# Starting a tile's first matrix product on six of its eight heads: fused top-k attention and two feed-forward networks on one Trainium2 core

## Chip, core and metric

The kernel runs on one core of a Trainium2 chip. The metric is device time in microseconds (us), the median of three runs; less is better. PE is the matrix engine, with PEld its weight loads; DVE, ACT and POOL are the vector, scalar and GpSimd engines, SP the engine that issues most DMAs. PE writes into PSUM banks, which DVE and ACT read; everything else lies in SBUF.

## What is computed

Two batches, 8 heads, 576 rows, head size 64. Each row keeps its 32 largest scores:

```python
scores = scale * np.matmul(q, k.transpose(0, 1, 3, 2))
kth = np.partition(scores, -top_k, axis=-1)[..., -top_k:-top_k + 1]
scores = np.where(scores >= kth, scores, -1000000000.0)
attn = np.exp(scores - np.max(scores, axis=-1, keepdims=True))
attn = attn / (np.sum(attn, axis=-1, keepdims=True) + 1e-09)
x = np.matmul(attn, v)                       # 1152 tokens x 512
h = x @ w1;  x = (np.maximum(h, 0) + np.log1p(np.exp(-np.abs(h)))) @ w2
h = x @ w3;  out = (np.maximum(h, 0) + alpha * np.minimum(h, 0)) @ w4
```

w1 and w3 are 512 x 2048, w2 and w4 2048 x 512. The weights arrive as 64-bit numbers.

## The kernel before

The 1152 tokens are nine tiles of 128 rows, taken in chunks `[[3], [4], [5], [6, 7, 8], [0, 1, 2]]`. The first three chunks are one tile each; their second network is computed together.

**Attention, by tile and head.** `scores` (L455) computes two heads at once on PE into PSUM banks, which ACT copies to SBUF (`s`, L476). `topk` (L485) ranks one head on DVE: four maxima of eight (L480) and three replacements between them (L483). ACT makes the negated, scaled maximum `nb` (L499) and a penalty for all that is under the 32nd value (L508, L509), POOL subtracts it in two halves (L514), and ACT takes the exponential and its sum (L516). `flip` transposes the result in 128x128 blocks on PE (L529, L535), ACT copies them (L532, L536), and `values` multiplies with v (L557). `finish` (L588) runs once all eight heads are there: the inverse sums are spread by POOL and four transposes (L604), and DVE multiplies them into the result (L612).

**Networks.** `Layer` goes through the 2048 hidden columns in 16 blocks of 128. `up` (L640) computes a block `ph` from four slices of x; for the first network ACT computes Abs, Exp and Ln (L663 to L665) and DVE adds (L666). `down` (L683) multiplies the block into `pa`. `up` is two blocks ahead of `down`. Chunks in `NATIVE` use fp32 products (L652, L698); the others split both operands into a high and a low part and use three products (L624 to L626).

**Weights.** `convert` (L341) loads 64-bit weights in two halves into one of `RAWB` raw buffers `cr` (L348), and DVE (L351, L354), ACT (L357, one per half) and POOL (L360, two per half) make 32-bit values `cx` of them. Each is stored to DRAM and loaded again for later chunks. There are 32 units of 1024 columns, sixteen for each network; 15 slots hold weights in SBUF.

**Order.** All operations are recorded with a number, and a table `ORDER` of these numbers, written into the file, is the order in which they are issued; each engine runs its own in that order. `fN` in the table stands for N filler products (L789) on the identity matrix, whose result nobody reads; a `b` behind a number chooses the second of two engines that an operation may run on.

PSUM has few banks: `pacc` 3, `pt` 2 (transposes, spread sums and, after the first tile, scores), `ph` 2, `pav` 1.

Of the kernel before, what the change touches and what calls it, by code (L numbers as in the profile page):

```python
# [18 lines left out]
P = 128  # L19
# [24 lines left out]
XNB = 1  # L44
# [3 lines left out]
RAWB = 2  # L48
RING = 15
NATIVE = {(0, 1), (0, 2), (1, 2), (0, 0)}  # L50
HOLD = {(0, 1): 2, (0, 2): 4}

# [104 lines left out]
109 431 f27 91 124 93 428 92 459 110 94 432 f4 97 125 111 458 118 441 99 112 98 144 100 126 113 135 145 101
127 442 114 146 128 446 158 129 f11 115 147 159 443 447 160 448 148 102 130 444 181 476 116 149 445 f14 131
182 161 133 150 475 460 449 132 151 162 134 f8 136 461 152 157 163 462 203 465 183 463 164 464 137 204 184 138
466 494 153 f10 139 477 467 174 185 141 140 478 468 f4 154 495 165 479 186 155 226 480 166 205 481 227 187 482  # L160
167 511 206 168 188 483 169 207 484 189 242 f26 170 172 485 228 171 190 512 173 208 243 f4 175 191 229 196 177
197 496 192 198 497 176 199 f2 178 209 498 230 219 501 499 210 231 500 179 180 244 502 f11 193 211 530 200 513
503 194 265 201 514 212 266 504 531 245 515 232 213 518 202 516 246 f18 380 517 214 381 233 519 374 547 382
# [136 lines left out]
def topk_attention_moe_kernel(ctx: ExitStack, tc: tile.TileContext, q, k, v, w1, w2, w3, w4, alpha, out):  # L300
# [541 lines left out]
```

## Time and profile before

| | us |
|---|---|
| median of three runs | 664.43 (663.53 to 664.88) |
| profiled execution, its own time | 661.64 |
| its span, first to last instruction | 659.8 |
| PE busy, of it fillers | 643.9, 59.5 |
| DVE busy | 542.9 |
| ACT busy | 496.9 |
| POOL busy | 377.0 |

The time of an execution is 1.8 us more than its span. Busy time of PE is modelled: a product's end overlaps the next one's start, so the distance between starts is the price of a product. The idle time given in front of an instruction names what ended it. The granted clock of the profile is a share of 2.4 GHz.

### The profile page before, as it was taken

The page shows a single profiled execution, that of the slowest core. Times are in us where ns is not written, and L with a number is a line of the kernel's source. Part 1 is how long each engine was busy: PE and PEld are TensorE (multiplying, and loading weights), DVE is VectorE, ACT ScalarE, POOL GpSimd, SP SyncE. Part 2 cuts the span into 40 slices and gives each one's busy share as a digit, 9 for nine tenths or more (in the row PEclk, how much of TensorE's full clock was granted, in tenths as well). Part 3 has the DMA queues.
Part 4 walks back from the last instruction along what each step waited for, and adds up shares of the span by engine and source line. Part 5 has one row for each costly group of instructions (what it writes and reads, how often), then busy time and mean ns, then how long its engine had stood idle before and what let it go on. Part 6 is the DMA issues. An engine that isn't in the chain of part 4 may idle for free.

```text
span 659.8 us, 12350 instructions
## 1 busy us (share of the span) xinstructions
PE 643.9 (98%) x4330; PEld 500.2 (76%) x4330; DVE 542.9 (82%) x1046; ACT 496.9 (75%) x1118; POOL 377.0 (57%) x402
## 2 busy tenths in 40 slices
PE   9999997999999899999999999999999999999997
PEld 7899765667677555555567788779898999999886
DVE  5999999999999999999998889999734654664632
ACT  4878898998799988788788889888545667673432
POOL 2566765642343677887585769886644343742520
PEclk9999999999999999999999999999999999999999
DMA  8765777740044379858424222221243433432501
GB/s 298 257 212 210 242 253 241 241 164 1 1 136 137 112 217 311 290 167 266 155 80 147 94 97 96 65 97 58 79 133 125 146 118 129 160 128 96 160 1 48
DMA packets 30159, 98.46 MB, mean 149 GB/s; under 512 B 3473, under 2 KB 4241, under 8 KB 30097
## 3 DMA queue, kind: packets, MB, share of 16 engines
q1 hardware_dynamic: 29952, 97.54, 45.2%
q8 instruction: 34, 0.56, 0.4%
q14 instruction: 29, 0.23, 0.1%
q10 hardware_dynamic: 144, 0.13, 0.1%
HBM read 78.52 MB, written 19.14 MB: 148 GB/s over the span
## 4 chain that ended last, share of the span: by engine, by line
PE 87%; issue 4%; POOL 3%; ACT 2%; DMA 2%; DVE 1%; SPq 0%; POOLq 0%; DVEq 0%
PE ph L652 11%; PE pa L698 10%; PE scrap L789 9%; PE ph L624 7%; PE pa L624 7%; PE ph L626 7%; PE ph L625 7%; PE pa L625 7%; PE pa L626 7%; PE pss L471 6%; PE pp L529 4%; POOL cx L360 2%; DMA cr<-in_w_dram 2%; POOL e L514 1%; PE pav__3750 L557 1%
## 5 line engine op out<-in xcount | busy, mean ns | idle before, releaser
L370 POOL TENSOR_TENSOR w<-w,wh 128x512 fp32r<-128x512 f32 x82 | 126.3, 1550 | 101.4 <-ACT wh L393 93.8
L514 POOL TENSOR_TENSOR e<-s,e 128x288 f32<-128x288 f32 x144 | 121.0, 860 | 64.4 <-ACT e L509 58.6
L480 DVE MAX8 m<-r 128x8 f32<-128x576 f32 x216 | 155.7, 747 | 0.1
L360 POOL TENSOR_TENSOR cx<-cx,cr 128x256 int32<-128x256 int32 x128 | 94.1, 762 | 62.2 <-ACT cr L357 60.5
L483 DVE MATCH_REPLACE8 r<-m,r 128x576 f32<-128x576 f32 x144 | 106.4, 742 | 0.0
L698 PE MATMUL pa<-cx,g 128*128 128x512 f32 x188 | 92.9, 604 | 2.3 <-DVE g L666 2.3
L357 ACT ACTIVATE cr<-cr 128x512 int16<-128x512 uint32 x64 | 82.5, 1378 | 4.4 <-DVE cr L354 4.0
L393 ACT CAST wh<-w 128x1024 fp32r<-128x1024 f32 x64 | 66.8, 1045 | 6.3 <-PE pa L624 2.0
L476 ACT COPY s<-pss 128x288 f32<-128x288 f32 x144 | 53.3, 407 | 21.7 <-PE pss L471 21.2
L480 DVE MAX8 m<-s 128x8 f32<-128x576 f32 x72 | 52.8, 749 | 10.6 <-ACT s L476 10.5
L789 PEld LDWEIGHTS scrap<-ident 128*128 128x128 f32 x474 | 55.9, 195 | 6.7 <-issue 5.3
L789 PE MATMUL scrap<-ident 128*128 128x128 f32 x474 | 59.5, 282 | 1.4 <-POOL ident masks.py:199 1.4
L516 ACT ACTIVATE e<-e,nb 128x576 f32<-128x576 f32 x72 | 55.8, 776 | 5.7 <-POOL e L514 5.5
L624 PE MATMUL pa<-w,gh 128*128 128x512 f32 x144 | 59.0, 409 | 0.0
L371 DVE TENSOR_TENSOR w<-w,wh 128x512 fp32r<-128x512 f32 x46 | 37.2, 811 | 26.4 <-ACT wh L393 24.8
L625 PE MATMUL pa<-wh,gl 128*128 128x512 f32 x144 | 56.8, 395 | 0.0
L626 PE MATMUL pa<-wh,gh 128*128 128x512 f32 x144 | 56.8, 395 | 0.0
L670 ACT ACTIVATE g<-ph 128x384 f32<-128x384 f32 x48 | 23.4, 490 | 43.7 <-PE ph L626 37.7
L471 PE MATMUL pss<-ks,q 64*64 64x288 f32 x576 | 53.1, 432 | 2.5 <-ACT pt L532 2.2
L672 DVE SCALAR_TENSOR_TENSOR g<-g,rest,ph 128x384 f32<-128x384 f32 x48 | 29.2, 608 | 31.8 <-ACT g L670 31.7
L371 DVE TENSOR_TENSOR gl<-g,gh 128x384 fp32r<-128x384 f32 x41 | 42.2, 1029 | 15.2 <-ACT gh L679 14.8
L652 PEld LDWEIGHTS ph<-xh,cx 128*128 128x128 f32 x336 | 42.0, 191 | 15.8 <-issue 8.2
(131 smaller groups left out, 1461.6 us busy)
## 6 DMA issues: line engine op xcount, KB each, us to landing
w<-ws SPq DMA_DIRECT2D x67, 512.0 KB, 3.3
cr<-in_w_dram SPq DMA_DIRECT2D x64, 512.0 KB, 5.5
ws<-cx SPq DMA_DIRECT2D x32, 512.0 KB, 6.6
v<-in_v_dram SPq DMA_DIRECT2D x12, 320.0 KB, 6.3
ks<-in_k_dram SPq DMA_DIRECT2D x11, 288.0 KB, 5.1
q<-in_q_dram SPq DMA_DIRECT2D x8, 256.0 KB, 5.3
out_dram<-o SPq DMA_DIRECT2D x8, 256.0 KB, 2.5
ks<-in_k_dram SPq DMA_DIRECT2D x2, 144.0 KB, 2.4
```

Source lines behind the costliest of these rows:

```text
L360: op("POOL", lambda part=part, r=r, cs=cs: nc.gpsimd.tensor_add(part().bitcast(I32)[:, cs], part().bitcast(I32)[:, cs], r().bitcast(I32)[: ...
L370: lambda: nc.gpsimd.tensor_sub(lo(), x(), hi().bitcast(F32)),
L471: nc.tensor.matmul(pss[n]()[part], qr()[head, pair, part], ks()[head, cs], start=True, stop=True)
L480: op("DVE", lambda: nc.vector.max(out=out(), in_=x()), reads=reads, writes=writes)
L483: op("DVE", lambda: nc.vector.match_replace(out=out(), in_to_replace=found(), in_values=x(), imm_value=LOWEST), reads=reads, writes=writes)
L514: op("POOL", lambda cs=cs: nc.gpsimd.tensor_sub(e()[:, cs], s()[:, cs], e()[:, cs]), reads=[s], writes=[e])
L624: nc.tensor.matmul(acc, ah, b_l, start=first, stop=False)
L625: nc.tensor.matmul(acc, a_l, bh, start=False, stop=False)
L626: nc.tensor.matmul(acc, ah, bh, start=False, stop=last)
L652: nc.tensor.matmul(hp(), w[0]().bitcast(F32)[:, cs], self.x[c][0]()[:, c, :], start=c == 0, stop=c == KT - 1)
L698: nc.tensor.matmul(acc(), gh()[:, cs], w[0]().bitcast(F32), start=first, stop=last)
L789: plan.emit(ORDER, lambda: nc.tensor.matmul(scrap()[:, :P], ident, ident, start=True, stop=True))
```

## The change

It begins the first network of tile 3 when six of its eight heads are ranked. `finish_part` takes over from `finish` for this tile, once after head 5 and once after head 7, each with its own sums, and writes three and then one of the four slices of x. `Layer.ahead` multiplies the first three slices with all 16 blocks of the first matrix, four blocks to a PSUM bank, and ACT copies the half sums to SBUF (`h`). Later `up_block` adds the half sum by a product with the identity, and the fourth slice.

For single tiles in fp32 (`wide`, two), two blocks of the first network share a PSUM bank and one set of activations of 256 columns. A third raw weight buffer is there. `nb` may be computed on POOL. Attention of the last chunk is recorded after the first network of the chunk before, and the last tile's results are copied in another split. The table is new: 239 fillers instead of 237, and 37 of the 72 `nb` on POOL; six of the low parts of `g` moved from DVE to POOL, four penalties from DVE to ACT.

```diff
-RAWB = 2
+RAWB = 3
+STREAM = 6
...
 ORDER = """
-4 2 5 3 12 364 363 386 387 240 f5 6 7 8 f1 9 11 10 19 96 56 f3 195 95 156 40 77 f4 13 26 41 117 14 0 42 27 15 f3
...
@@ topk
-        if h == 0:
+        if h == 0 or streamed(ci) and h == STREAM:
...
-        op("ACT", lambda: nc.scalar.mul(nb(), m()[:, 0:1], -SCALE), reads=[m], writes=[nb])
+        op(("ACT", "POOL"), (lambda: nc.scalar.mul(nb(), m()[:, 0:1], -SCALE), lambda: nc.gpsimd.tensor_scalar(
+            nb(), m()[:, 0:1], -SCALE, None, op0=ALU.mult)), reads=[m], writes=[nb])
@@ values
+        if streamed(ci):
+            if h in (STREAM - 1, H - 1):
+                finish_part(ci, t, h)
+        elif h == H - 1:
             finish(ci, ti, t)
+    def finish_part(ci, t, h):
+        lo = STREAM if h == H - 1 else 0
+        n = h + 1 - lo
+        ks = slice(lo // 2, (h + 1) // 2)
...
+        op("POOL", lambda: nc.gpsimd.tensor_copy(
+            rx()[:, lo:h + 1], rs()[:, lo:h + 1].unsqueeze(2).broadcast_to([P, n, D])), reads=[rs], writes=[rx])
+        op("PE", spread, reads=[rx], writes=[pr])
+        op("ACT", lambda: nc.scalar.copy(xn()[:, cols], pr()[:, cols]), reads=[pr], writes=[xn])
+        op("DVE", lambda: nc.vector.tensor_tensor(
+            x()[:, ks].rearrange("p k n -> p (k n)"), av()[:, cols], xn()[:, cols], op=ALU.mult),
...
@@ Layer.__init__
+            self.wide = GROUP if self.native and layer == 0 and self.n == P else 1
+            self.early = streamed(ci) and layer == 0
+            if self.early:
+                self.sums = [buf("row", OB, [P, DM], F32, f"h{i}") for i in range(FJ // 4)]
+                for j in range(FJ):
+                    if j % GROUP == 0:
+                        fetch((layer, j // GROUP, 0), j, ci, True)
+                    if j % 4 == 0:
+                        z = bank("pacc", 3, 4 * P, f"pe{j // 4}")
+                    self.ahead(j, z)
+        def ahead(self, j, z):
+            lo = j % 4 * P
+            self.products(j, j, z, slice(lo, lo + P), 0, STREAM // 2, [z], True)
+            if j % 4 == 3:
+                o = self.sums[j // 4]
+                op("ACT", lambda: nc.scalar.copy(o(), z()),
+                   reads=[z], writes=[Half(o, i * P, i * P + P) for i in range(4)])
+        def up_block(self, j, at):
+            n, nm, ci = self.n * self.wide, f"{self.layer}{self.ci}_{j}", self.ci
+            if self.early:
+                hp, o = bank("ph", 2, n, f"ph{nm}"), self.sums[j // 4]
+                for i in range(self.wide):
+                    k, cols = (j + i) % 4 * P, slice(i * P, (i + 1) * P)
+                    self.products(j + i, at + i, hp, cols, STREAM // 2, KT, [hp], False, Half(o, k, k + P))
+                self.activate(j, at, n, nm, ci, hp, [hp])
+                return
...
@@ products, called by ahead and up_block
+                    if base is not None:
+                        nc.tensor.matmul(hp()[:, cols], ident, base(), start=True, stop=False)
...
@@ the loop over chunks
-        if ci + 1 < len(CHUNKS):
+        follows = ci + 1 < len(CHUNKS) and min(len(CHUNKS[ci]), len(CHUNKS[ci + 1])) > 1
+        if ci + 1 < len(CHUNKS) and not follows:
             attend(first_row[ci + 2] - 1)
         for layer in (0, 1) if among[ci][-1] == ci else (0,):
+            if layer and follows:
+                attend(first_row[ci + 2] - 1)
```

Three places of the issue order, as the built programs have it. Names carry numbers of buffers: `pp`, `pq` are transposes of ranked heads, `pss` scores, `pr` spread sums, `pav` values, `ph`, `pa` blocks and sums of a network, `pe` half sums, `py` the transposed output of the first network, `cr` raw and `cx` converted weights.

**PE, the end of tile 3's attention**, around the spread of its sums (`pr`). Before:

```order
L789 MATMUL scrap<-ident 128x128 x11
L529 MATMUL pp_883<-ident,e_71 128x128 x4
L604 MATMUL pr__893<-ident,rx_847 128x128 x4
L789 MATMUL scrap<-ident 128x128 x18
L652 MATMUL ph_1_939<-xh_917,cx_208 128x128 x4
L652 MATMUL ph_0_948<-xh_917,cx_208 128x128 x4
L535 MATMUL pq_962<-ident,e_71 128x128
L529 MATMUL pp_966<-ident,e_71 128x128 x4
```

and in the change, from just ahead of the transposes of tile 3's last two heads on:

```order
L875 MATMUL scrap<-ident 128x128 x6
L527 MATMUL pp_763<-ident,e_72 128x128 x4
L613 MATMUL pr__772<-ident,rx_696 128x128 x3
L875 MATMUL scrap<-ident 128x128 x7
L727 MATMUL pe_797<-xh_785,cx_343 128x128 x3
L527 MATMUL pp_804<-ident,e_72 128x128 x4
L533 MATMUL pq_810<-ident,e_72 128x128
L727 MATMUL pe_797<-xh_785,cx_343 128x128 x3
L727 MATMUL pe_797<-xh_785,cx_472 128x128 x6
L727 MATMUL pe_830<-xh_785,cx_220 128x128 x6
L727 MATMUL pe_830<-xh_785,cx_249 128x128 x6
L727 MATMUL pe_858<-xh_785,cx_519 128x128 x6
```

Fillers before the first products went from 18 to 7, and the products of the first three slices stand there, ahead of tile 3's last values; other fillers stand later.

**ACT, the same stretch**, from the last transposes of tile 3 on. Before:

```order
L532 COPY pt_74<-pp_796 128x512
L536 COPY pt_74<-pq_801 128x128
L499 ACTIVATE nb_811<-m_768 128x1
L476 COPY s_835<-pss_820 128x288
L516 ACTIVATE e_71,sum_841<-e_71,nb_639 128x576
L476 COPY s_845<-pss_817 128x288
L357 ACTIVATE cr_699<-cr_699 128x512 x2
L476 COPY s_845<-pss_851 128x288
L476 COPY s_835<-pss_854 128x288
L508 ACTIVATE kb_888<-m_683 128x1
L509 ACTIVATE e_71<-s_555,kb_888 128x576
L532 COPY pt_73<-pp_883 128x512
```

and in the change:

```order
L354 ACTIVATE cr_590<-cr_590 128x512 x2
L694 COPY h_836<-pe_797 128x512
L534 COPY pt_74<-pq_810 128x128
L354 ACTIVATE cr_670<-cr_670 128x512 x2
L694 COPY h_864<-pe_830 128x512
L506 ACTIVATE kb_871<-m_707 128x1
L507 ACTIVATE e_71<-s_564,kb_871 128x576
L530 COPY pt_74<-pp_804 128x512
L694 COPY h_896<-pe_858 128x512
L473 COPY s_911<-pss_890 128x288
L473 COPY s_914<-pss_893 128x288
```

Two conversions (four halves) and the half sums stand close together, and by the end of the piece ACT has done eighteen halves, where it had done sixteen.

**PE and ACT, the start of the second network for tiles 3 to 5.** PE before:

```order
L578 MATMUL py_2722<-ident,o_2690 128x128 x4
L529 MATMUL pp_2738<-ident,e_72 128x128 x4
L652 MATMUL ph_1_2749<-yh_1704,cx_2692 128x384 x4
L652 MATMUL ph_0_2780<-yh_1704,cx_2692 128x384 x4
L529 MATMUL pp_2803<-ident,e_72 128x128 x4
L535 MATMUL pq_2811<-ident,e_72 128x128
L652 MATMUL ph_3_2813<-yh_1704,cx_2247 128x384 x4
```

PE in the change:

```order
L580 MATMUL py_2526<-ident,o_2518 128x128 x4
L556 MATMUL pav__2112<-pt_74,v_1434 64x128 x10
L468 MATMUL pss_2552<-ks_747,q_1692 64x288 x2
L468 MATMUL pss_2555<-ks_747,q_1692 64x288 x2
L727 MATMUL ph_0_2561<-yh_1621,cx_2160 128x384 x2
L727 MATMUL ph_1_2568<-yh_1621,cx_2160 128x384 x4
L468 MATMUL pss_2587<-ks_747,q_1692 64x288 x2
L468 MATMUL pss_2590<-ks_747,q_1692 64x288 x2
L727 MATMUL ph_0_2561<-yh_1621,cx_2160 128x384 x2
L641 MATMUL pr__2607<-ident,rx_2488 128x128 x4
L527 MATMUL pp_2616<-ident,e_71 128x128 x4
L727 MATMUL ph_3_2623<-yh_1621,cx_2213 128x384 x4
L527 MATMUL pp_2648<-ident,e_71 128x128 x4
```

ACT in the change, from the copy of `py` on:

```order
L585 COPY yh_1621<-py_2526 128x4x128
L354 ACTIVATE cr_2327<-cr_2327 128x512 x2
L514 ACTIVATE e_71,sum_2490<-e_71,nb_2393 128x576
L473 COPY s_2571<-pss_2555 128x288
L473 COPY s_2575<-pss_2552 128x288
L354 ACTIVATE cr_2418<-cr_2418 128x512 x2
L748 ACTIVATE g_1_2597<-ph_1_2568 128x384
L473 COPY s_2571<-pss_2590 128x288
L473 COPY s_2575<-pss_2587 128x288
L354 ACTIVATE cr_2467<-cr_2467 128x512 x2
L748 ACTIVATE g_0_2632<-ph_0_2561 128x384
L496 ACTIVATE nb_2638<-m_2627 128x1
L530 COPY pt_73<-pp_2616 128x512
```

The transposes `pp` no longer follow `py` directly: values, scores and two of the second network's blocks come between, and ACT does six conversion halves there.

## Rows read from the trace of the kernel before

**Rows 1.** The page's head and its busy time, share and instructions by engine.

```profile
span 659.8 us, 12350 instructions
...
PE 643.9 (98%) x4330; PEld 500.2 (76%) x4330; DVE 542.9 (82%) x1046; ACT 496.9 (75%) x1118; POOL 377.0 (57%) x402
```

**Rows 2.** The page's costliest groups: busy us, mean ns, then idle before.

```profile
L789 PE MATMUL scrap<-ident 128*128 128x128 f32 x474 | 59.5, 282 | 1.4 <-POOL ident masks.py:199 1.4
```

**Rows 3.** Windows by stage, three answers; columns as in the first line.

```profile
core 0: us, PE busy (x) PEld busy (x) DVE busy (x) ACT busy (x) POOL busy (x), PEclk, DMA share, GB/s
...
78.00:125.00 47.00, 39.22 (x383) 26.73 (x384) 45.88 (x100) 43.51 (x111) 31.34 (x42) 1.00 0.78 253
...
235.00:505.00 270.00, 269.68 (x1615) 192.11 (x1614) 237.95 (x462) 215.39 (x462) 194.25 (x201) 1.00 0.45 146
...
53.00:80.00 27.00, 26.94 (x261) 24.17 (x260) 26.64 (x55) 21.49 (x42) 19.10 (x24) 1.00 0.72 240
80.00:140.00 60.00, 52.26 (x481) 35.41 (x480) 58.88 (x129) 57.23 (x152) 37.49 (x49) 1.00 0.76 243
...
80.00:114.10 34.10, 27.98 (x284) 18.97 (x283) 32.98 (x71) 32.37 (x86) 21.53 (x28) 1.00 0.77 251
```

**Rows 4.** The chain that ended last: start us, us, what, with its count of records.

```profile
150.77 0.86 PE pa L698 x2
...
154.39 1.24 PE pav__1588 L557 x20
...
158.67 0.65 PE pss L471 x8
...
160.82 0.87 PE pp L529 x8
...
181.67 1.78 PE ph L652 x16
...
253.24 2.58 PE ph L652 x8
```

**Rows 5.** Timeline of PE, two waits: start us, us, instruction, [idle before <-releaser].

```profile
113.14 1.05 PE L652 MATMUL ph<-xh,cx 128*128 128x128 f32 x7 [2.19 <-DVE g L666]
...
229.72 0.63 PE L529 MATMUL pp<-ident,e 128*128 128x128 f32 x4 [2.04 <-ACT s L476]
```

**Rows 6.** Windows of 1 us around the clock's fall, columns as in rows 3.

```profile
230.00:231.00 1.00, 1.00 (x6) 0.59 (x4) 1.00 (x2) 1.00 (x2) 1.00 (x2) 0.91 0.00 0
231.00:232.00 1.00, 1.00 (x3) 0.67 (x2) 1.00 (x5) 0.97 (x4) 0.86 (x2) 0.50 0.00 0
```

**Rows 7.** Timeline: PE's last transpose of three pairs of heads, and DVE's last maximum.

```profile
114.14 0.27 PE L535 MATMUL pq<-ident,e 128*128 128x128 f32 x1
...
132.07 1.40 DVE L480 MAX8 m<-r 128x8 f32<-128x576 f32 x2
...
140.14 0.27 PE L535 MATMUL pq<-ident,e 128*128 128x128 f32 x1
...
221.86 0.27 PE L535 MATMUL pq<-ident,e 128*128 128x128 f32 x1
```

**Rows 8.** Groups of ACT from 78 to 145 us by shape, then three of the whole run.

```profile
L357 ACT ACTIVATE cr<-cr 128x512 int16<-128x512 uint32 x14 | 18.0, 1381 | 1.5 <-DVE cr L354 1.3
L532 ACT COPY pt<-pp 128x512 f32<-128x512 f32 x11 | 6.6, 603 | 0.2
...
L663 ACT ACTIVATE g<-ph 128x128 f32<-128x128 f32 x19 | 5.0, 282 | 1.3 <-PE ph L652 1.3
...
L499 ACT ACTIVATE nb<-m 128x1 f32<-128x1 f32 x11 | 2.3, 209 | 0.0
...
L670 ACT ACTIVATE g<-ph 128x384 f32<-128x384 f32 x48 | 23.4, 490 | 43.7 <-PE ph L626 37.7
...
L514 POOL TENSOR_TENSOR e<-s,e 128x288 f32<-128x288 f32 x144 | 121.0, 860 | 64.4 <-ACT e L509 58.6
...
L829 POOL MEMSET const-float32-1.0<- 128x1 f32 x1 | 0.1, 98 | 0.0
```

More of the change, by code (lines that the diff above doesn't have):

```diff
@@ L157 @@
[L157 to L161, printed above, removed]
@@ L487, in topk @@
         ci, ti, t, h = rows[i]
-        if h == 0:
-            tiles[t]["sum"] = buf("sum", 2, [P, H], F32, f"sum{t}")
-        total = tiles[t]["sum"]
+        if h == 0 or streamed(ci) and h == STREAM:
+            tiles[t]["sum"] = buf("sum", 2, [P, H], F32, f"sum{t}{h}")
+        total = work[i]["sum"] = tiles[t]["sum"]
         s = work[i].pop("s")
@@ L547, in values @@
         av, pts = tiles[t]["av"], pt_tiles[i // 2 % PB]
+        o0 = h // 2 * P
         pt = pts[0].tile
@@ L558, in products @@
                                          start=c == 0, stop=c == 4)
-        op("PE", products, reads=[*pts] + [vt for vt, _, _ in parts], writes=[av])
-        if h == H - 1:
+        op("PE", products, reads=[*pts] + [vt for vt, _, _ in parts], writes=[Half(av, o0, o0 + P)])
+        if streamed(ci):
+            if h in (STREAM - 1, H - 1):
+                finish_part(ci, t, h)
+        elif h == H - 1:
             finish(ci, ti, t)
     def features(name, ci, layer):
-        tag = name + str(ci % 2) * (not layer)
         n = sum(len(CHUNKS[c]) for c in (among[ci] if layer else [ci])) * P
+        tag = name + (f"s{ci % 2}" if n == P else "") * (not layer)
         if (layer, ci) in NATIVE:
@@ L586, in to_features, with streamed, spread @@
                reads=[pp, hi], writes=[lo])
+    def streamed(ci):
+        return ci == 0 and STREAM
+    def finish_part(ci, t, h):
+        lo = STREAM if h == H - 1 else 0
+        n = h + 1 - lo
+        ks = slice(lo // 2, (h + 1) // 2)
+        if not lo:
+            x = features("x", ci, 0)[0]
+            xs[ci] = [(x, f"x{c}") for c in range(KT)]
+        x = xs[ci][0][0]
+        av, total = tiles[t]["av"], work[rows.index((ci, 0, t, h))]["sum"]
+        rs = buf("rs", 2, [P, H], F32, f"rs{t}{h}")
+        op("DVE", lambda: nc.vector.tensor_scalar(rs()[:, lo:h + 1], total()[:, lo:h + 1], 1e-9, None, op0=ALU.add),
+           reads=[total], writes=[rs])
+        op("DVE", lambda: nc.vector.reciprocal(rs()[:, lo:h + 1], rs()[:, lo:h + 1]), writes=[rs])
+        xn = buf("xn", XNB, [P, DM], F32, f"xn{t}{h}")
+        rx = buf("rx", 1, [P, H, D], F32, f"rx{t}{h}")
+        pr = bank("pt", 2, KT * P, f"pr{t}{h}_")
+        cols = slice(ks.start * P, ks.stop * P)
+        def spread():
+            for c in range(ks.start, ks.stop):
+                nc.tensor.transpose(pr()[:, c * P:(c + 1) * P], rx()[:, 2 * c:2 * c + 2, :].rearrange("p a b -> p (a b)"), ident)
+        op("POOL", lambda: nc.gpsimd.tensor_copy(
[4 more added lines that the diff above has]
+            x()[:, ks].rearrange("p k n -> p (k n)"), av()[:, cols], xn()[:, cols], op=ALU.mult),
+           reads=[Half(av, c * P, c * P + P) for c in range(ks.start, ks.stop)] + [xn] + [x] * (lo > 0),
+           writes=[f"x{c}" for c in range(ks.start, ks.stop)] + [x] * (lo == 0))
     def finish(ci, ti, t):
@@ L591, in finish @@
         av, total = tiles[t]["av"], tiles[t]["sum"]
+        avs = [Half(av, o, o + P) for o in range(0, KT * P, P)]
         parts, cs = xs[ci], slice(ti * P, (ti + 1) * P)
@@ new lines, in ahead @@
+        def ahead(self, j, z):
[5 more added lines that the diff above has]
+                   reads=[z], writes=[Half(o, i * P, i * P + P) for i in range(4)])
+        def up(self, j, at):
+            if at % self.wide:
+                return
+            self.up_block(j, at)
+        def up_block(self, j, at):
[6 more added lines that the diff above has]
+                self.activate(j, at, n, nm, ci, hp, [hp])
+                return
+            hp = bank("ph", 2, n, f"ph{nm}")
+            for i in range(self.wide):
+                self.products(j + i, at + i, hp, slice(i * self.n, (i + 1) * self.n), 0, KT, [hp])
+            self.activate(j, at, n, nm, ci, hp, [hp])
@@ L644, in up, with products @@
+        def products(self, j, at, hp, cols, c_lo, c_hi, writes, ahead=False, base=None):
+            n, ci = self.n, self.ci
             w = [x.parts[j % GROUP] for x in ready[self.layer, j // GROUP, 0]]
-            hp = bank("ph", 2, n, f"ph{nm}")
-            step = 1 if at == 0 and self.x[0] is not self.x[-1] else 2
-            for c0 in range(0, KT, step):
+            step = c_hi - c_lo if ahead else 1 if at == 0 and self.x[0] is not self.x[-1] or (c_hi - c_lo) % 2 else 2
+            for c0 in range(c_lo, c_hi, step):
@@ L651, in products, with activate @@
                         if self.native:
-                            nc.tensor.matmul(hp(), w[0]().bitcast(F32)[:, cs], self.x[c][0]()[:, c, :],
-                                             start=c == 0, stop=c == KT - 1)
+                            nc.tensor.matmul(hp()[:, cols], w[0]().bitcast(F32)[:, cs], self.x[c][0]()[:, c, :],
+                                             start=base is None and c == 0, stop=c == c_hi - 1)
                         else:
                             xh, xl, *_ = self.x[c]
-                            three(hp(), w[0]()[:, cs], w[1]()[:, cs], xh()[:, c, :], xl()[:, c, :],
+                            three(hp()[:, cols], w[0]()[:, cs], w[1]()[:, cs], xh()[:, c, :], xl()[:, c, :],
                                   c == 0, c == KT - 1)
-                op("PE", products,
-                   reads=w + [x for c in range(c0, c0 + step) for x in self.x[c][-2:]], writes=[hp])
+                op("PE", products if not ahead else lambda f=products: f(),
+                   reads=w + [x for c in range(c0, c0 + step) for x in self.x[c][-2:]] + [base] * (base is not None),
+                   writes=writes)
+        def activate(self, j, at, n, nm, ci, hp, made):
             g = buf("g", GB, [P, n], F32, f"g{nm}")
             if self.layer == 0:
-                op("ACT", lambda: nc.scalar.activation(g(), hp(), AF.Abs), reads=[hp], writes=[g])
+                op("ACT", lambda: nc.scalar.activation(g(), hp(), AF.Abs), reads=made, writes=[g])
                 op("ACT", lambda: nc.scalar.activation(g(), g(), AF.Exp, scale=-1.0), writes=[g])
@@ L724, in down @@
             half = DM // 2
-            for o, acc in zip(os, self.acc):
-                if self.layer == 1 and ci == len(CHUNKS) - 1:
-                    op("ACT", lambda o=o, acc=acc: nc.scalar.copy(o()[:, :half], acc()[:, :half]),
-                       reads=[acc], writes=[Half(o, 0, half)])
-                    z = o if o is not os[-1] else buf("row", OB, [P, DM], F32, f"oz{nm}")
-                    op("DVE", lambda z=z, acc=acc: nc.vector.tensor_copy(
-                        z()[:, half:], acc()[:, half:]), reads=[acc], writes=[Half(z, half, DM)])
-                else:
-                    op("ACT", lambda o=o, acc=acc: nc.scalar.copy(o(), acc()), reads=[acc],
-                       writes=[Half(o, 0, half), Half(o, half, DM)])
+            final = self.layer == 1 and ci == len(CHUNKS) - 1
+            for i, (o, acc) in enumerate(zip(os, self.acc)):
+                whole = [Half(o, 0, half), Half(o, half, DM)]
+                if not final or i == 0:
+                    op("ACT", lambda o=o, acc=acc: nc.scalar.copy(o(), acc()), reads=[acc], writes=whole)
+                elif i < len(os) - 1:
+                    op("DVE", lambda o=o, acc=acc: nc.vector.tensor_copy(o(), acc()), reads=[acc], writes=whole)
+                else:
+                    t, z = self.tiles[i], buf("row", OB, [P, DM], F32, f"oz{nm}")
+                    op("ACT", lambda o=o, acc=acc: nc.scalar.copy(o()[:, :half], acc()[:, :half]),
+                       reads=[acc], writes=whole)
+                    op("ACT", lambda t=t, o=o: nc.scalar.dma_start(out[t * P:(t + 1) * P, :half], o()[:, :half]),
+                       reads=whole)
+                    op("DVE", lambda z=z, acc=acc: nc.vector.tensor_copy(z()[:, half:], acc()[:, half:]),
+                       reads=[acc], writes=[Half(z, 0, half), Half(z, half, DM)])
+                    op("SP", lambda t=t, z=z: nc.sync.dma_start(out[t * P:(t + 1) * P, half:], z()[:, half:]),
+                       reads=[Half(z, 0, half), Half(z, half, DM)])
             for ti, (t, o) in enumerate(zip(self.tiles, os)):
@@ L737, in down @@
                     to_features(o, bank("pacc", 3, 512, f"py{nm}{ti}"), ys[group[-1]][0], before + ti)
-                elif ci < len(CHUNKS) - 1 or o is not os[-1]:
+                elif not final or ti < len(os) - 1:
                     op("SP", lambda t=t, o=o: nc.sync.dma_start(out[t * P:(t + 1) * P, :], o()),
                        reads=[Half(o, 0, half), Half(o, half, DM)])
-                else:
-                    op("ACT", lambda t=t, o=o: nc.scalar.dma_start(out[t * P:(t + 1) * P, :half], o()[:, :half]), reads=[Half(o, 0, half)])
-                    op("SP", lambda t=t, z=z: nc.sync.dma_start(out[t * P:(t + 1) * P, half:], z()[:, half:]), reads=[Half(z, half, DM)])
     steps = []
```

183 lines of the change are left out of this document (112 added, 71 removed), and 103 rows, old and new, of the table ORDER.

## The prediction

> **What bounds the kernel now.** I read the page's busy table first. PE is busy 98% of the span [rows 1], but 59.5 us of that is work that computes nothing: 237 filler products, two records each [rows 2]. The windows by stage [rows 3] show the rest. The fillers stand before 78 us, where DVE still ranks the scores. From 78 to 125 us PE is idle 47.00 - 39.22 = 7.8 us, in waits like the 2.19 us one in [rows 5]. From 235 to 505 us it is idle 0.3 us in 270 [rows 3], so every microsecond won or lost before that arrives at the end whole. There is one more loss: at 229.72 PE has waited 2.04 us for ACT's copy of scores [rows 5], and the granted clock, 1.00 until 230, is then 0.50 (1.2 instead of 2.4 GHz) until past 234. One window at 0.91, three at 0.50 and one at 0.88 (the first two are in [rows 6]) cost 0.09 + 1.50 + 0.12 = 1.7 us. That place loses 2.04 + 1.7 = 3.75 us. So the bound is PE's order of work, held up by ACT and DVE between 78 and 235 us.
>
> **The change, part by part.** PE prices are starts, not the modelled ends: a 128-column fp32 product costs 2 x 0.111 = 0.222 us, a 512-column one 0.86, a 384-column one 2 x 0.3225 = 0.645, ten value products 1.24, four score products 0.65, a transpose 0.109 [rows 4].
>
> *Added PE work.* Sixteen products add the saved half sums back into PSUM: 16 x 0.222 = 3.6 us. Two fillers more: 0.4 us. All other products are the same in number. Together +4.0 us, and since PE has no idle time after 235 us nothing covers them there.
>
> *Where PE stands.* I compare at one point, the transposes of heads 2 and 3 of tile 5, at 140.14 before [rows 7]. Up to it the order of the change has 88 products of the first matrix instead of 74 (+3.1 us), one 512-column product more (+0.86), the sixteen additions and the two fillers: +8.0 us of PE work. So behind it stands 4.0 us less than before. When is the point reached? Three bounds:
> - PE alone: 140.1 - 7.8 of waits + 8.0 = 140.3.
> - DVE: its last maximum for this pair ends at 133.5 [rows 7]. Its order now holds one more replacement before that and wider additions, about 1 us more; subtracting on POOL and two ACT steps take another 4 us: not before 138.5.
> - ACT: by the transposes of heads 6 and 7 of tile 4 (114.14 before, [rows 7]) it has five more halves of weight conversions, 5 x 18.0/14 = 6.4 us, four copies of half sums at 0.60, one more copy of transposes 0.60 and one more ranked head 1.0, less seven small scalings at 0.21 that moved to POOL [rows 8]. Its activations come out even: 30 of 128 columns before, 22 of 256 now, which I put half way from 0.28 for 128 to 0.49 for 384 columns [rows 8]. That is +9.0 us. ACT worked 32.4 us between 80 and 114.1 [rows 3]; 32.4 + 9.0 at its share of 57.2/60 between 80 and 140 takes 43.4 us, so 123.4. PE's products from there to the point come to 18.4 us in the new order; from 140.14 to 221.86 before [rows 7] products of 77.5 us took 81.7, of which 0.6 was idle, so 4.5% more: 19.2 and 142.6.
>
> I take 141.9, near ACT's bound, because ACT has the least room there. That is 1.8 later than before, with 4.0 less to do.
>
> *The loss at 229.* Before, these transposes (heads 2 and 3 of tile 7) stand right behind the last ones of the first network's output. In the new order 5.2 us of the second network's 384-column products and 3 us of other work come between, and the pair of heads ahead of them already stands behind 19.5 us more of PE work, so what DVE ranks for them is done in time. But ACT now has six conversion halves (7.7 us) in the stretch that follows, and about 5.8 us of smaller work: 13.5 us, against 11.2 us of PE work up to the second set of transposes there, which needs a PSUM buffer that ACT empties. The new wait lies between 0 and 2.3 us; I take 1.4, since ACT starts this stretch with some lead.
>
> *At nothing.* The third raw buffer lets weight loads start earlier; but DVE, which takes them up, is busy 58.9 of the 60 us from 80 to 140 [rows 3], so at most 1.1 us of waiting for them can go there, and PE gains it only where DVE is its bound, which it isn't above. The 37 scalings moved to POOL: the nearest rows are a 128x1 memset of 0.098 us and the subtraction of 288 columns, 0.86 [rows 8], so 3.6 to 32 us of POOL, which is idle 43% of the span [rows 1]; I take the low end, by size. They stand in front of subtractions of older heads, and wait for DVE instructions one or two ahead: cover is DVE's backlog. Six low parts moved from DVE to POOL, in a stretch in which neither holds PE. The last copies are split anew over ACT and DVE; within 0.3 us either way.
>
> **Sum.** +1.8 - 4.0 - (3.75 - 1.4) = -4.55 us on the profiled execution (span 659.8, time 661.64). That one lies 2.8 us under the median of 664.43; the difference carries over: **659.9 us**. A measurement can tell 0.2%, 1.3 us, from no change.
>
> **Rivals.**
> 1. *No new wait.* The point at 140.3 and no loss in the second network: +0.2 - 4.0 - 3.75 = -7.55, 656.9 us. For it: in the old order PE waits 0.3 us in the 270 after 235 [rows 3], so waits are no rule there. Against: ACT's queue, as above. Chance 0.14.
> 2. *PE has room.* If added products slip into time in which PE only seems busy, the 4.0 us cost nothing: -8.55, 655.9 us. For it: weight loads fill 192 of 270 us between 235 and 505 [rows 3]. Against: a pair of 512-column records takes its 0.86 us from start to start [rows 4], with nothing left between. The Trainium skill (Perfetto Trace Analysis, Identifying the Most-Contended Engine) calls matmul busy time a poor measure of room on TensorE and wants the busy share of weight loads instead. By that rule 29% of this stretch would be free, and this rival would hold. Chance 0.08.
> 3. *The loss in the second network returns whole*: a wait of 2.3 us and the clock at half again, 1.7, with the point at ACT's 142.6: +2.5 - 4.0 - 3.75 + 4.0 = -1.25, 663.2 us, no change that can be told. For it: the conversions are packed there, and a wait of 2.04 us was enough before. Chance 0.15.
> 4. *ACT falls behind between 80 and 125 us*, slower than before. The scores, transposes and spread sums rotate through two PSUM buffers that ACT empties, so PE waits for ACT, and ACT for PE. If ACT reaches only its share of 53 to 80 us, 21.5/27 = 0.80 [rows 3], its 41.4 us take 51.8: 131.8, the point at 151.0, and +10.9 - 4.0 - 2.35 = +4.55, 669.0 us. It decides at a share of 0.88, where the sum is nought. For it: nine more microseconds in the same queue. Against: the share was low at 53 to 80 because ACT had nothing to do. Chance 0.18.
>
> **Numbers.** The forecast has 0.45; with rivals 1 and 2 faster has 0.67, rival 3 is no change 0.15, slower 0.18. The range starts under rival 2, at 655.5, and ends at 667, an ACT share of 0.83; it leaves out the end of rival 4 and little below.
>
> **What would show it.** Right: the transposes of heads 2 and 3 of tile 5 at 140 to 143 us; idle of PE between 78 and 142 under 5 us; the granted clock at 1.00 past 220, or a dip that follows a wait near the second network's start; products after that point without gaps; 16 more products of 0.222 us. The forecast fails if that point comes after 146 us with ACT under 0.88 busy from 80 us on (rival 4), if a wait of over 4 us stands behind 235 us, or if the added products don't lengthen PE's work (rival 2).

## The result and the profile after

The changed kernel takes 672.40 us (median of 4 runs, 671.23 to 673.55), the kernel before on the same chip 664.65 (4 runs, 663.53 to 665.37): ratio 1.0131, interval 1.0107 to 1.0155. It is slower; the forecast was 659.9 us and its range ended at 667.0. The profiled execution took 673.37 us, span 671.6: 11.7 us more than the one of before, where the medians differ by 7.75.

These lines of the page of the changed kernel (its head, the busy time, and the fillers' group) are to be set beside [rows 1, 2].

```profile
span 671.6 us, 12322 instructions
...
PE 646.3 (96%) x4366; PEld 505.3 (75%) x4366; DVE 537.9 (80%) x1014; ACT 488.7 (73%) x1021; POOL 396.3 (59%) x446
...
L875 PE MATMUL scrap<-ident 128*128 128x128 f32 x478 | 61.2, 284 | 1.3 <-POOL ident masks.py:199 1.3
```

Work did not grow on DVE or ACT; PE lost time. Windows of the changed kernel, columns as in [rows 3]:

```profile
78.00:125.00 47.00, 34.42 (x302) 27.16 (x301) 33.85 (x70) 31.86 (x69) 23.86 (x35) 0.85 0.65 211
80.00:100.00 20.00, 8.50 (x85) 7.64 (x85) 13.64 (x28) 6.96 (x14) 5.90 (x7) 0.66 0.53 171
...
235.00:505.00 270.00, 264.91 (x1649) 185.53 (x1648) 247.25 (x475) 215.75 (x464) 193.92 (x221) 1.00 0.40 130
```

From 78 to 125 us PE is idle 12.6 us instead of 7.8, and in 80 to 100 every engine stands: DVE, full before [rows 3], has 13.64 of 20. PE's three largest waits in the whole run (waited for: us in total, times, longest):

```profile
PE pav__1010 L556 <- DVE xh L619: 11.5, 1, 11.5
PE ph L727 <- DVE g L750: 1.8, 1, 1.8
PE pp L527 <- ACT s L473: 1.5, 3, 0.6
```

One wait of 11.5 us stands out. The timeline around it, in the order PE, DVE, ACT (start us, us, instruction, [idle before <-releaser]):

```profile
92.97 2.40 PE L556 MATMUL pav__1010<-pt,v 128*64 128x64 f32 x40 [11.50 <-DVE xh L619]
95.30 3.18 PE L875 MATMUL scrap<-ident 128*128 128x128 f32 x16
98.41 0.71 PE L468 MATMUL pss<-ks,q 64*64 64x288 f32 x8
...
91.98 0.75 DVE L477 MAX8 m<-r 128x8 f32<-128x576 f32 x1
92.65 0.27 DVE L619 TENSOR_TENSOR xh<-pav__442,xn 128x128 f32<-128x128 f32 x1
92.84 0.07 DVE L480 MATCH_VALUE_LOAD r<-m,r 128x8 f32 x1
92.91 0.73 DVE L480 MATCH_REPLACE8 r<-m,r 128x576 f32<-128x576 f32 x1
102.80 1.42 DVE L477 MAX8 m<-s 128x8 f32<-128x576 f32 x2 [9.16 <-ACT s L473]
...
78.62 0.27 ACT L618 COPY xn<-pr__975 128x128 f32<-128x128 f32 x1 [0.19 <-PE pr__975 L613]
99.24 0.70 ACT L473 COPY s<-pss 128x288 f32<-128x288 f32 x2 [12.26 <-PE pss L468]
```

The rows read like this. Tile 4's first value products (pav__1010) want the one PSUM bank for value sums, in which tile 3's still stand (pav__442). The last reader is the DVE multiplication for tile 3's heads 6 and 7, a step the change split off. Its other operand xn was copied by 78.89 us, but on DVE fourteen ranking steps of tile 4's heads and six conversion instructions still stand ahead of it, and it runs at 92.65. PE stands from 81.47 on. The scores of the next heads are behind the value products on PE, so ACT gets none to copy (12.26 us) and DVE, once through its queue, none to rank (9.16 us). When PE goes on it has half its clock (granted 0.50, 1.2 GHz): 40 value products take 2.40 us, where experiment 1 below shows the same 40 in 1.39 at 1.00.

In the kernel before, one multiplication ended the whole tile, well ahead of the next tile's value products:

```profile
76.11 0.69 DVE L612 TENSOR_TENSOR xh<-pav__419,xn 128x512 f32<-128x512 f32 x1
...
83.15 1.03 PE L557 MATMUL pav__1001<-pt,v 128*64 128x64 f32 x28
```

The next rows are the transposes of three pairs of heads in the changed kernel: heads 2 and 3 of tile 4, heads 6 and 7 of it, and heads 2 and 3 of tile 5. Before, the last two were at 114.14 and 140.14 [rows 7].

```profile
106.90 0.27 PE L533 MATMUL pq<-ident,e 128*128 128x128 f32 x1
...
133.76 0.27 PE L533 MATMUL pq<-ident,e 128*128 128x128 f32 x1
...
154.82 0.27 PE L533 MATMUL pq<-ident,e 128*128 128x128 f32 x1
```

So the point of comparison comes at 154.82 instead of the predicted 141.9.

### The profile page after: what moved, and what is told of

The parts are those of the page before. It is cut to its first block, busy times and chain, and to the rows that moved or that the text cites. A ratio compares the mean times of both kernels' runs of the same rounds, so it can differ in the third digit from the quotient of the medians.

```text
span 671.6 us, 12322 instructions
## 1 busy us (share of the span) xinstructions
PE 646.3 (96%) x4366; PEld 505.3 (75%) x4366; DVE 537.9 (80%) x1014; ACT 488.7 (73%) x1021; POOL 396.3 (59%) x446
## 4 chain that ended last, share of the span: by engine, by line
PE 76%; ACT 11%; DVE 6%; issue 4%; POOL 2%; DMA 1%; SPq 0%; POOLq 0%; DVEq 0%; ACTq 0%
PE pa L777 9%; PE ph L727 8%; PE ph L661 7%; PE scrap L875 7%; PE ph L662 7%; PE ph L663 7%; PE pa L661 6%; PE pa L663 6%; PE pa L662 6%; PE pss L468 5%; ACT cr L354 3%; PE pp L527 3%; DVE m L477 2%; DVE r L480 2%; ACT e L507 1%
## 5 line engine op out<-in xcount | busy, mean ns | idle before, releaser
L367 POOL TENSOR_TENSOR w<-w,wh 128x512 fp32r<-128x512 f32 x82 | 124.0, 1520 | 95.1 <-ACT wh L390 87.1
L512 POOL TENSOR_TENSOR e<-s,e 128x288 f32<-128x288 f32 x144 | 119.1, 844 | 64.3 <-ACT e L507 42.0
L357 POOL TENSOR_TENSOR cx<-cx,cr 128x256 int32<-128x256 int32 x128 | 104.0, 834 | 42.3 <-ACT cr L354 35.4
L354 ACT ACTIVATE cr<-cr 128x512 int16<-128x512 uint32 x64 | 84.5, 1379 | 8.0 <-DVE cr L351 7.8
L875 PE MATMUL scrap<-ident 128*128 128x128 f32 x478 | 61.2, 284 | 1.3 <-POOL ident masks.py:199 1.3
L875 PEld LDWEIGHTS scrap<-ident 128*128 128x128 f32 x478 | 57.6, 198 | 6.5 <-issue 5.0
L507 ACT ACTIVATE e<-s,kb 128x576 f32<-128x576 f32 x68 | 52.8, 777 | 2.3
L777 PEld LDWEIGHTS pa<-cx,g 128*128 128x128 f32 x192 | 32.5, 190 | 28.6 <-issue 23.2
```

The costliest lines, as they stand in the source:

```text
L354: op("ACT", lambda r=r: nc.scalar.activation(r().bitcast(I16)[:, :, 2], r()[:, :, 0], AF.Copy, scale=2.0 ** -29), reads=[part], writes=[r])
L357: op("POOL", lambda part=part, r=r, cs=cs: nc.gpsimd.tensor_add(part().bitcast(I32)[:, cs], part().bitcast(I32)[:, cs], r().bitcast(I32)[: ...
L367: lambda: nc.gpsimd.tensor_sub(lo(), x(), hi().bitcast(F32)),
L512: op("POOL", lambda cs=cs: nc.gpsimd.tensor_sub(e()[:, cs], s()[:, cs], e()[:, cs]), reads=[s], writes=[e])
L777: nc.tensor.matmul(acc(), gh()[:, cs], w[0]().bitcast(F32), start=first, stop=last)
L875: plan.emit(ORDER, lambda: nc.tensor.matmul(scrap()[:, :P], ident, ident, start=True, stop=True))
```

## The experiments

In the expectations theory A is the explanation just given, or the one that the prediction stands on; rivals B and C are others.

**1. The multiplication early.** One number of the table, the late multiplication's 208, moves:

```diff
-238 476 f3 223 200 565 254 224 518 f3 221 529 222 271 f4 247 530 ...
+238 476 f3 223 200 565 254 224 518 f3 221 529 222 208 271 f4 247 530 ...
-... 278 572 f10 260 208 555 603 293 262 483 569 604
+... 278 572 f10 260 555 603 293 262 483 569 604
```

> The changed kernel with one table entry moved: the DVE multiplication that ends tile 3's heads 6 and 7 (xh<-pav,xn 128x128) stands 19 DVE instructions earlier, right behind the conversion that began at 79.45 us, instead of at 92.65 us; xn was there at 78.89. Theory A, the single pav bank is freed late by DVE's own order: PE's wait of 11.5 us before tile 4's first value products shrinks to under 1 us, DVE's idle time of 9.2 us behind it goes too, the transposes of heads 2 and 3 of tile 4 (106.9 before this edit) come at 94 to 98, and 671.6 us becomes 659 to 662. Rival B, DVE or ACT is simply late by that much and the wait only shows it: the same time is waited for at the next transposes, which stay at 103 or later, and the whole at 669 or more. Rival C, PE is let through and then waits for first layer weights whose raw loads are late: a wait on cx or cr of several us at 95 to 110, and 664 to 667.

659.77 us (6 runs, 658.09 to 660.46), ratio to before 0.9933 (0.9906 to 0.9961). Windows and rows of PE in this kernel (the last three are again the transposes of the three pairs):

```profile
80.00:100.00 20.00, 18.71 (x224) 16.37 (x226) 20.00 (x40) 18.20 (x39) 14.87 (x20) 1.00 0.88 308
...
80.00:123.40 43.40, 41.36 (x383) 30.05 (x382) 42.97 (x88) 41.50 (x91) 31.82 (x44) 1.00 0.83 290
...
82.26 1.39 PE L556 MATMUL pav__1011<-pt,v 128*64 128x64 f32 x40
83.58 2.05 PE L875 MATMUL scrap<-ident 128*128 128x128 f32 x16
85.56 0.72 PE L468 MATMUL pss<-ks,q 64*64 64x288 f32 x8
...
94.44 0.27 PE L533 MATMUL pq<-ident,e 128*128 128x128 f32 x1
...
121.33 0.27 PE L533 MATMUL pq<-ident,e 128*128 128x128 f32 x1
...
142.38 0.27 PE L533 MATMUL pq<-ident,e 128*128 128x128 f32 x1
```

This is theory A, number for number: the wait is gone, DVE is full, the transposes of heads 2 and 3 of tile 4 come at 94.44, and the kernel becomes 0.7% faster than the one before. One instruction's place on DVE was worth 12.6 us. The wait is 11.5 of it, and the clock adds 2.1: from the value products to the scores PE needs 98.41 - 92.97 = 5.44 us in the changed kernel and 85.56 - 82.26 = 3.30 here, for the same work. The point of comparison differs by 154.82 - 142.38 = 12.4, about 1 us less than these two together. Most of that is no gain: this profile came to the value products 0.8 us later, at 82.26 where PE began to wait at 81.47 in the other.

**2. Half as far.** The same number leaves its old place as in experiment 1, but goes here:

```diff
-532 289 288 240 f8 226 257 273 550 533 290 274 241 228 ...
+532 289 288 240 f8 226 257 273 550 533 290 274 208 241 228 ...
```

> The same DVE multiplication moved only half as far: it stands behind the second maximum of head 4 of tile 4, where DVE was at 86.6 us in the changed kernel. Theory A: PE's wait before tile 4's first value products is 5 to 6 us instead of 11.5, and the time lies 5 to 6 us under the changed kernel's, 665 to 667 us. Rival B (the wait only shows a lateness of DVE or ACT): within 1 us of the changed kernel, 671 to 673.

665.99 us (10 runs, 665.04 to 668.35). PE's longest wait is:

```profile
PE pav__1010 L556 <- DVE xh L619: 6.1, 1, 6.1
```

Waits of 11.5, 6.1 and 0 us go with 672.4, 666.0 and 659.8: the time follows the wait, a little over 1 us for each microsecond of it. Rival B falls.

**3. The cure on PE.** The multiplication stays late; the value products (247) go behind the next scores:

```diff
-... 221 529 222 271 f4 247 530 272 239 534 255 531 548 535 287 285 256 549
+... 221 529 222 271 f4 530 272 239 534 255 531 548 535 287 256 549
-... 291 553 536 f9 229 275 242 585 231 537 567 230
+... 291 553 536 f9 229 247 285 275 242 585 231 537 567 230
```

> The changed kernel with the cure on PE instead of DVE: the late multiplication stays where it is (it ran at 92.65 us), but tile 4's first value products, which need the pav bank that it frees, stand behind the scores of heads 6 and 7 of tile 4 with their fillers instead of ahead of them (the load of v into their buffer follows them). Theory A, an order of PE in which scores stand behind a product that cannot start yet starves ACT and DVE: PE still waits 7 to 9 us for the bank, but the scores are there when DVE comes to them, DVE's 9.2 us of idle time at 93.6 go, the transposes of heads 2 and 3 of tile 4 come at 96 to 99 instead of 106.9, and the time is 661 to 665 instead of 672.4. Rival B, what counts is PE's own lost time: 8 of 11.5 us stay lost and the time is 668 to 670. Rival C, the load queue behind that load of v is held up, and weights come late: a wait on cr of several us between 95 and 120, 666 or more.

666.72 us (10 runs, 665.24 to 668.77), between theory A's figures and rival B's; the transposes of heads 2 and 3 of tile 4 come at 103.06, not 96 to 99. The timeline (PE, then DVE):

```profile
88.68 0.71 PE L468 MATMUL pss<-ks,q 64*64 64x288 f32 x8 [1.49 <-ACT s L473]
94.08 2.40 PE L556 MATMUL pav__1080<-pt,v 128*64 128x64 f32 x40 [4.68 <-DVE xh L619]
96.42 3.70 PE L875 MATMUL scrap<-ident 128*128 128x128 f32 x16
...
101.28 0.69 DVE L348 TENSOR_SCALAR cx<-cr 128x1024 uint32<-128x1024 uint32 x1 [3.15 <-DMA cr<-in_w_dram]
```

DVE is no longer starved of scores, as A has it. Its one wait here is 3.15 us for a raw transfer, rival C's sign, and the time is in C's range too. But PE goes from 94.08 to the transposes without a gap, so that wait does not make them late. The time still follows PE's own loss, as B has it, only that the loss is smaller than B reckoned. Against experiment 1 PE loses 1.49 - 0.23 for scores, 4.68 for the bank, and by the half clock 2.40 - 1.39 and 3.70 - 2.05: 8.6 us together, and the transposes are 103.06 - 94.44 = 8.6 late. So feeding ACT and DVE was worth less than letting PE go on; theory A had that share wrong.

**4. Without the fillers behind it.** On experiment 1, the fillers f8, f9, f8 and f10 are struck out of the two table lines that begin with 532 and 554.

> The kernel with the multiplication moved early, and without the four runs of fillers (8, 9, 8 and 10, some 4.1 us at 0.117 each) that stand on PE between tile 4's first value products and its next transposes. If PE's own work sets the pace behind the cured wait, the time falls by up to 4 us more, to 655 to 658. If the ranking on DVE and the copies on ACT set it, the fillers only fill waits: within 1 us of the kernel with the multiplication moved early. If the granted clock falls in the emptier stretch (under 1.00 between 80 and 110 us), it is 1 to 2 us slower than that kernel.

660.15 us (8 runs, 659.32 to 661.31): no difference that can be told from experiment 1. The expectation put too little on these fillers: f8 is sixteen records of PE (above, at 83.58), and at the 0.117 us that the expectation reckoned with, but for each record, the 35 fillers are about 8.2 us, not 4.1. Even so they only covered waits. Without them PE waits 5.0 us for ACT's copies of scores and 3.3 for its exponentials in the whole run, where experiment 1 has 1.2 and 0.2. The granted clock from 80 to 100 us is 0.74 and the point of comparison comes at 144.05, 1.7 us later, but from 230.3 us on the two traces lie within 0.2 us of each other. What takes the 1.7 us up is PE's wait at 230: 0.7 us in this profile, 2.5 in experiment 1's (see 6).

**5. More work on PE.** On experiment 1, one transpose is issued 41 times:

```diff
-nc.tensor.transpose(pq(), e.tile[:, 4 * P:5 * P], ident)
+[nc.tensor.transpose(pq(), e.tile[:, 4 * P:5 * P], ident) for _ in range(41 if (t, h) == (8, 1) else 1)]
```

> On top of the multiplication moved early: one transpose of tile 8's heads 0 and 1 (pq, at 302.31 us) is issued 41 times instead of once, 40 x 0.109 = 4.4 us more work on PE, and nothing else. Theory A, behind the point at 142 us PE's own work sets the end, as the prediction's sum takes it: 3.3 to 4.4 us slower than 659.8 (PE's waits of 1.0 at 340 to 360 and 0.8 at 440 to 460 may take up some of it). Rival B, the ranking on DVE sets the pace of the attention up to 475 us, and PE has room there: at most 1 us slower.

662.52 us (10 runs, 661.98 to 664.49): 2.75 more, under theory A's 3.3 and far over rival B's 1. The profiles show where the rest is. The added records:

```profile
299.60 4.64 PE L533 MATMUL pq<-ident,e 128*128 128x128 f32 x41
304.08 1.88 PE L777 MATMUL pa<-cx,g 128*128 128x512 f32 x4
```

They begin 302.31 - 299.60 = 2.71 us earlier than in experiment 1's profile and span 658.5 becomes 660.2: 1.7 + 2.7 = 4.4 us, the added work whole, from there to the end. The 2.7 us are from before it: 0.8 were there at the point of comparison (141.54), and 1.9 come from the wait at 230, 0.6 us in this profile and 2.5 in that of experiment 1. Other profiles agree: from the product that ends this wait to the end of the span, those of experiments 1 to 4 and 7 all take 428.1 us, this one 660.2 - 227.74 = 432.5.

**6. The conversion behind.** On experiment 1, conversion 1561/1562 and one of its halves on ACT go behind three ranking steps (1072, 1073, 1056), the activation of the first hidden block (1445) and the product of the second (1450):

```diff
-1527 1069 1531 1443 1541 1532 1040 1070 1447 1001 1528 1054 1000 1575 1542 1561 1448 1529 1055 1545 1002 1543
-1071 1533 1574 1449 1444 1562 1544 1004 1003 1072 1566 1023 1546 1450 1595 1017 1073 1563 1480 ...
-1596 1056 1445 1481 ...
+1527 1069 1531 1443 1541 1532 1040 1070 1447 1001 1528 1054 1000 1575 1542 1448 1529 1055 1545 1002 1543
+1071 1533 1574 1449 1444 1544 1004 1003 1445 1023 1546 1072 1073 1056 1450 1561 1562 1566 1595 1017 1563 1480 ...
+1596 1481 ...
```

> On top of the multiplication moved early: at the start of the second network the conversion of one block of its up weights (cx<-cr, cr<-cr) stands on DVE behind three ranking steps and the product g of the second hidden block instead of ahead of them, and on ACT the activation of the first hidden block stands ahead of that block's two conversion halves. In the kernel with the multiplication early DVE waited 2.54 us at 226.12 for that block's raw transfer (issued 217.32, there at 226.09), and PE waited 2.50 us at 230.44 for the product behind it. Theory A, a late raw transfer held DVE in order and through it PE: PE's wait at 230 falls to under 0.5 us and the time by 1.5 to 2.5 us, to 657.3 to 658.3. Rival B, the two hidden blocks are late for their own copies and activations on ACT: PE's wait stays 2 us or more and the time within 0.7 us of 659.8. Rival C, the conversion that now comes later is waited for a little behind: the wait at 230 goes, another of as much comes before 260, and the time stays at 659.8.

659.24 us (6 runs, 658.96 to 659.44), no difference that can be told from experiment 1's 658.09 to 660.46. PE's wait for g is gone, and one of 1.6 us for ACT stands beside its place (pp <- ACT kb): rival C in kind. But that wait is only 0.6 us in other profiles without this edit (experiment 5's, for one), so a single profile does not show what the edit did. The wait it was aimed at, in experiment 1, on PE and on DVE:

```profile
230.44 2.85 PE L727 MATMUL ph<-yh,cx 128*128 128x384 f32 x8 [2.50 <-DVE g L750]
...
226.12 1.03 DVE L348 TENSOR_SCALAR cx<-cr 128x1024 uint32<-128x1024 uint32 x1 [2.54 <-DMA cr<-in_w_dram]
```

That raw transfer, 512 KB, was issued from 217.32 to 217.65 and landed 8.4 us after that, at 226.09, the slowest of ten between 205 and 236 us; their median was 6.7. In experiment 5's profile the slowest took 7.4 and DVE waited for none.

**7. The scaled maxima on ACT again.** On experiment 1, the 37 b marks of the nb steps are taken off.

> On top of the multiplication moved early: all 37 scaled maxima nb that the change put on POOL are on ACT again, as before the change. The prediction put their move at nothing. Theory A: within 1 us of 659.8, since ACT has room for 37 x 0.1 us (4 us over 400). Rival B, ACT's order is the near bound between 80 and 125 us, where four of them stand, and around 230: 1 to 3 us slower.

659.60 us (4 runs, 659.40 to 659.79): their move is worth nothing either way, as predicted.

**8. All of 1, 6 and 7 together.**

> The multiplication early, the conversion block at 226 us behind the ranking steps and the hidden block on DVE (and its halves behind the activation on ACT), and the 37 scaled maxima nb on ACT: the three edits that each cost nothing or gained something. Expected from the runs of each: 658.6 to 659.6 us (659.77 with the first alone, 659.24 with the first two, 659.6 with the first and third). Rival, they spoil one another on ACT around 230: over 660.

659.95 us (6 runs, 659.36 to 660.94), a little over what was expected and under the rival's 660; its ratio to before is 0.9932, experiment 1's 0.9933. So the one move of experiment 1 is what beats both kernels, by 0.7% the one before, and nothing is added to it.

**9. Two raw buffers.** On experiment 1:

```diff
-RAWB = 3
+RAWB = 2
```

with 60 raw loads and one DVE conversion later in the table.

> The kernel with the multiplication moved early, and the third raw weight buffer taken away (RAWB 2 as before the change). Every engine keeps its order but for one conversion of DVE and the load queue: 60 raw loads are issued later, each when one of two buffers is free. The prediction put the third buffer at nothing. Theory A, it is worth nothing, as two buffers served before the change: within 1 us of 659.8. Rival B, the changed order counts on weights that come one block earlier: DVE or POOL waits for cr several times, 2 to 8 us slower, with the waits in the first 130 us or at 217 to 260.

697.97 us (4 runs, 697.36 to 700.30), ratio to before 1.0510 (1.0486 to 1.0533), 38.2 us over experiment 1. DVE's group for the conversion here:

```profile
L348 DVE TENSOR_SCALAR cx<-cr 128x1024 uint32<-128x1024 uint32 x32 | 25.1, 783 | 40.4 <-DMA cr<-in_w_dram 40.1
```

and in experiment 1:

```profile
L348 DVE TENSOR_SCALAR cx<-cr 128x1024 uint32<-128x1024 uint32 x32 | 24.9, 780 | 2.5 <-DMA cr<-in_w_dram 2.5
```

This is far beyond rival B's 8 us: with two buffers DVE stands 16 times for a raw transfer in the new order. What a third buffer does for the old order was not tried. Nor were the parts of the change taken singly: experiment 1 shows what the whole is worth with one step moved, not what starting on six heads alone is worth.

## Why the prediction was wrong

The profiles of before, after and experiment 1, split as the sum was (the point is heads 2 and 3 of tile 5; the last three rows are for the stretch from there to the end):

| us | before | after | exp. 1 |
|---|---|---|---|
| point reached | 140.14 | 154.82 | 142.38 |
| from there to the end | 519.7 | 516.7 | 516.1 |
| PE busy in it | 512.9 | 507.3 | 506.9 |
| of it lost to half clock | 1.7 | 0 | 0 |
| PE idle in it | 6.8 | 9.3 | 9.2 |

- **When is the point reached.** This step failed: 141.9 predicted, 154.82 measured, 12.9 us. The three bounds were sums of work for PE, DVE and ACT. None asked whether the order lets an engine do its work. PE's bound took the old 7.8 us of waits out and put no new one in, ACT's took for granted that ACT is fed, DVE's counted its instructions up to the point, not which of them PE waits for. What the runs showed in their place is PE's wait of 11.5 us for one DVE instruction and 2.1 us of half clock behind it; with that instruction moved the point came at 142.38. The one pav bank, its new last reader and that reader's place on DVE could all be read from the changed order before any run. I wrote "cover is DVE's backlog" for the scalings; the same backlog delays whatever is put behind it.
- With that instruction moved the number was good: the point at 142.38 (141.9 forecast, ACT's bound 142.6), with 3.25 us of PE's idle time from 78 to 142. Its two parts were off both ways: heads 6 and 7 of tile 4 came at 121.33, 2.1 us before ACT's 123.4, and from there to the point it took 21.05 us instead of 19.2. ACT was as full as its bound had it, 41.50 of 43.40 us from 80 to 123.4, but "ACT has the least room there" was wrong: DVE was busy 42.97. So it is partly luck that ACT's bound fits.
- **Four us less work behind the point.** Right: 512.9 - 1.7 - 506.9 = 4.3 us in experiment 1, 3.9 in after. That such work arrives at the end (rival 2 denied it) is what experiment 5's 4.4 us say. The Trainium skill (Perfetto Trace Analysis, Identifying the Most-Contended Engine) judges room on TensorE by MFU and by the weight loads' busy share. The second of these is not borne out here: the loads fill 191.69 of 270 us from 235 to 505 in experiment 1, about the share of [rows 3], and experiment 5's added transposes were still paid whole.
- **The loss at 229.** This was half right. The half clock is gone, and the new wait at the second network's start is 1.8 us in after and 0.6 to 2.5 in experiments 1 to 5 and 7 (1.4 predicted, 0 to 2.3). But what makes it long is not ACT's six halves: ACT itself stood 2.73 us until 229.17 in experiment 1, behind DVE. Where DVE stood 2.54 us for a raw transfer (experiment 1) or 1.94 (after), PE waited 2.5 and 1.8, and where DVE stood 0.5 or less, 0.6 to 0.7. And the sum had no other new wait behind the point. Experiment 1 has five more of 0.5 to 0.8 us there, 3.1 together, where the kernel before had two, 0.9 together. So PE is idle 2.4 us more behind the point (3.6 to 3.9 us of the table's idle time lie behind its last product), where the sum had 0.64 less. From profile to profile experiment 1 gains 659.8 - 658.5 = 1.3 us, where the sum had 4.55.
- **The medians.** Experiment 1's, 659.77, is on the forecast, and partly by luck: its own profile lies 0.6 us above its median (660.32), that of before 2.8 below (661.64 against 664.43). I let that difference "carry over"; it does not, and these 3.4 us cover the 3.2 that the sum had too much. Why the profile of before is so far from its median, in runs from 661.17 to 666.70, stays open; transfers that land early or late, as at 230, are a candidate that was not tested.
- **Every microsecond before 235 arrives whole.** Right, but for the raw transfer at 230. Against experiment 5's profile, which did not wait for one, experiments 2, 3 and 4 reach the point 7.4, 9.5 and 2.5 us later, and the product behind the wait at 230 just as much later. The 1.7 us that vanish between experiments 1 and 4 are experiment 1's own wait for a late transfer.
- **At nothing.** nb on POOL: right (experiment 7), though the 37 of them take 0.22 us each in experiment 1, 8.1 us of POOL and not the low end of 3.6. The third raw buffer: "at most 1.1 us" was reckoned on the old order, and the new order depends on it for 38 us (experiment 9). That cost the forecast nothing, since the buffer was there, but the reason given did not bear on the new order.
- **Rival 4** had slower at 669.0 with the point at 151.0, near what came, by another mechanism: ACT did not fall behind, it stood idle (busy 6.96 of 20 us from 80 to 100). Its sign was met all the same, the point after 146 us with ACT under 0.88 busy (43.07 of 60 us from 80 to 140): a low share does not tell an engine that falls behind from one that isn't fed.

## What to carry to other kernels

When an order is written anew, go through every buffer of which there is one: find its last reader, count what stands ahead of that reader on its engine, and compare with when the next writer is due. Sums of busy time per engine can't see this; one short instruction behind 13 us of full queue cost more than all the added work. And a buffer that seems idle in the old order may be what the new order stands on.

## What the hardware showed unexpectedly

- PE's clock. In after, PE stood from 81.47 to 92.97 us, and the granted clock was 0.50 (1.2 GHz) from 85 to 97. But in experiment 1 an idle stretch of 2.50 us left it at 1.00 (2.4 GHz), and before one of 2.19 us did [rows 3, 5], where 2.04 us were followed by 0.50 [rows 5, 6]. Two windows of after, then three of experiment 1:

```profile
93.00:94.00 1.00, 1.00 (x20) 1.00 (x22) 0.64 (x1) 0.00 (x0) 0.00 (x0) 0.50 0.00 0
...
98.00:99.00 1.00, 1.00 (x13) 0.49 (x11) 0.00 (x0) 0.00 (x0) 0.00 (x0) 1.00 0.72 127
...
229.00:230.00 1.00, 0.00 (x0) 0.00 (x0) 1.00 (x4) 0.83 (x1) 0.00 (x0) 1.00 1.01 410
230.00:231.00 1.00, 0.56 (x2) 0.43 (x3) 1.00 (x3) 1.00 (x2) 0.41 (x1) 1.00 1.01 369
231.00:232.00 1.00, 1.00 (x5) 0.60 (x4) 1.00 (x3) 1.00 (x4) 0.59 (x2) 1.00 0.99 266
```

The length of a wait alone does not tell here whether the clock falls.

- Transfers of 512 KB, ten of them between 205 and 236 us, landed 4.7 to 8.4 us after issue in experiment 1 and 3.8 to 7.4 in experiment 5, with the same program in that stretch. Between these two profiles PE's wait at the second network's start differs by 1.9 us, and DVE's wait for such a transfer is there in the first only.
